# A fused attention and gated MLP kernel: every pair of head groups runs its sums and values together, and the whole written order is replaced

## The chip, the cores and the metric

The kernel runs on one core of one Trainium2 chip. The metric is the device time of one execution in microseconds (us). Three runs of the kernel before took 283.26, 287.59 and 288.25 us, so the median is 287.59 us and the runs differ by 1.7% among themselves. One further execution was recorded by the hardware profiler; its records span 282.1 us.

A core has five engines, each with a queue of its own: TensorE (PE, with weight loads as PEld), VectorE (DVE), ScalarE (ACT), GpSimd (POOL) and SyncE (SP), which here only issues transfers. Transfers between the outer memory, SBUF and back are done by 16 DMA engines.

## The reference

`B=8` batches, `H=12` heads, `S=448` positions, head dimension `D=64`. All inputs and the output are float32.

```python
q_n, k_n = rmsnorm(q, g_q), rmsnorm(k, g_k)        # x / sqrt(mean(x*x) + 1e-6) * g
scores = 1/sqrt(64) * q_n @ k_n.T                   # (8, 12, 448, 448)
attn = softmax(scores)
x = (attn @ v).transpose(0, 2, 1, 3).reshape(8, 448, 768)

h = maximum(x @ w_in, 0)                            # w_in (768, 1024)
u, v = h[..., :512], h[..., 512:]
v_n = (v - mean(v)) / sqrt(var(v) + 1e-6)           # over the 512
v_s = einsum('ts,bsd->btd', w_spatial, v_n) + b_spatial[None, :, None]
out = (u * v_s) @ w_out                             # w_out (512, 768)
```

## The kernel before

**Groups and units.** Four heads of one batch make a group `G`; there are 24 groups, three to a batch. A group's q, k or v is one tile of 128 partitions (two heads of 64 partitions, seven positions in each) by 2 x 448 numbers, 448 KB. A group's scores are made in seven units; a unit fills two PSUM banks with 128 x 448 numbers each.

**The order is written out by hand.** The string `PLAN` holds some 1,700 words. Each word is one step, `name.arguments/slots/engine`, and the loop at the end of the kernel (L722 to L725) calls `op_<name>` for each word. The scheduler of the language is off, so each engine runs its instructions in the order in which the words stand. What an engine does next is therefore fixed; a late operand holds everything behind it on the same engine. Waits are put in from the tiles that an instruction reads and writes. `SLOTS` (L160) says how many buffers of each kind there are; the slot numbers in the words choose among them. SP's transfers are issued in the order of the words as well.

**The words, in the order of the work of a group:**

- `L` loads q, k or v (L298; v of a group in the second half position goes in two halves, L304). `Q` squares (L391, L393), `R` sums the squares over a head (L404), `I` and `J` make 1/rms with a logarithm and an exponential on ACT (L417, L422), `N` multiplies (L437), on POOL or DVE. For group 0 the same steps exist by halves: `l q r i j n`.
- q and k must then be turned. `T` does it as a transposing transfer from SP (L492), after which k gets its factor g in `Z` (L473 on ACT, L475 on DVE). Or `P` does it on the PE (L456; `p` by halves, L464), and `K` (`k`) copies PSUM to SBUF, with the factor g for k.
- `S` makes the scores of one unit, eight matmuls of 64 x 32 weights (L517), which stand on eight different parts of the PE array. `E` is the exponential of a unit (L525, ACT), two banks at once.
- `s`, `a` and `b` are the passes: sums of the exponentials by a column of ones, and the two halves of the values (L550). A pass over one unit of one group is four matmuls of 64 x 32 weights. `flip` (L314) decides on which half of the partitions a group's heads lie. With groups below `SINGLES` (4) the flip is 0 and each pass is issued alone. From group 4 on, odd groups are flipped, and a pass of an even group and of the odd one after it are issued together (last argument 1): eight matmuls on eight parts of the array.
- `D` and `d` make 1/sum on ACT (L569, L573), `X` multiplies the values by it into `xt` (L579).
- For a batch: `V` and `U` are the two halves of x @ w_in (L595, L661), each in three steps of two matmuls; `c` and `u` the maximum with 0 (L586 on ACT, L588 on DVE); `B`, `M`, `m`, `A` the normalisation (L636, L637, L642, L645, L652); `H` the spatial product (L675), `G` the product with u (L680), `O` the last product (L689), `o` its copy to SBUF (L372 ACT, L374 DVE), `t` the store. `W` does the last 64 rows of V of a batch and of O of the batch before (L624).

**The weights.** `wi` loads w_in in eight transfers from POOL (L332), each 32 partitions of all three column groups; no `U` or `V` is placed before all eight. `ws` loads w_spatial early (L336); it is turned on the PE by `Y` (L359) and copied by `y`. `wb` and `wx` bring the bias into the last row.

**The factor g.** `gl` loads g_q and g_k as two rows into one partition, issued by SP behind the loads of group 0 (L307). `gA` multiplies them (L378), `gB` turns the row into a column with a small float32 matmul (L383), `gC` copies the column to `g2_col` (L386). Every `k`, `K` and `Z` reads `g2_col`.

**Fill work.** `z` issues matmuls of the identity (L263), 159 in all in 42 words, each of 64 columns, written into the unused 64 columns of PSUM bank 7.

Of the kernel before, what the change touches and what calls it, by code (L numbers as in the profile page):

```python
# [9 lines left out]
FP = mybir.dt.float32  # L10
# [26 lines left out]
S.2.3/34 E.2.1/h/a s.0.3.0 L.5.1/5 s.1.6.0 wi.0.0//g F.1//v P.3.1/7 P.3.0/6 E.2.3/i/a D.0/0/a Q.4.1/1/v R.4.1//v
I.4//a S.2.6/34 F.2//g b.1.3.0/0 b.1.0.0 D.1/1/a b.1.4.0 b.1.6.0 K.3.0/3/v wi.1.0//g s.2.1.0/6 b.1.2.0 d.0//a
b.2.1.0/5 E.2.6/j/a b.2.3.0 Q.5.1/0/g K.3.1/3/v J.4//a b.2.2.0 a.1.6.0/7 L.5.0/6 Q.5.0/2/a X.0.0//v N.4.1/2/g d.1//a
a.1.4.0 a.1.0.0 R.5.1//v a.2.3.0/4 N.4.0/3/g S.2.4/23 E.2.4/k/a R.5.0//v I.5//a b.2.5.0 b.1.1.0 b.2.0.0 X.0.1//v  # L40
a.2.6.0 b.1.5.0 s.2.0.0 a.2.5.0 J.5//a X.1.1//v a.1.1.0 S.3.0/23 E.3.0/l/a s.2.2.0 s.2.4.0 s.2.6.0 s.2.5.0 s.2.3.0
a.1.2.0 b.2.4.0 D.2/0/a S.3.3/01 E.3.3/9/a S.3.5/23 a.1.5.0 a.2.4.0 Q.6.0/1/g a.1.3.0 b.2.6.0 X.1.0//v E.3.5/1/a
a.2.0.0 N.5.0/0/g d.2//a N.5.1/1/g z.0/f a.2.1.0 a.2.2.0 R.6.0//v S.3.2/01 S.3.1/67 U.0.0.0/3 U.0.3.1/2 U.0.0.1
X.2.0//v V.0.0.1/4 L.6.1/8 Q.6.1/0/a X.2.1//v U.0.3.0 L.8.1/7 T.4.1/0 V.0.1.0/5 Z.4/0/v E.3.1/c/a Q.8.1/2/g E.3.2/2/a
U.0.0.2 u.0.0//a T.4.0/0 S.4.3/67 E.4.3/a/a R.6.1//v L.7.0/4 S.3.4/01 E.3.4/0/a V.0.0.2 I.6//a V.0.1.1 V.0.0.0
c.0.0//v V.0.1.2 c.0.1//v U.0.3.2 S.4.1/67 J.6//a S.4.4/01 S.4.5/34 wx//a W.0/5 E.4.1/8/a B.0.0//v S.4.2/67 u.0.3//v
Q.7.0/1/g E.4.4/b/a L.3.2/2 S.3.6/01 U.0.2.1/2 E.4.5/4/a N.6.1/2/g U.0.1.2/4 U.0.2.2 E.4.2/5/a U.0.2.0 T.5.0/1 F.3//v
S.4.6/67 s.3.2.0/3 E.3.6/f/a E.4.6/g/a s.3.5.0 T.5.1/1 Z.5/1/v c.0.3//v N.6.0/3/g S.5.1/01 s.3.0.0 u.0.2//v E.5.1/i/a
s.3.4.0 a.3.0.0/2 S.5.6/67 R.7.0//v E.5.6/7/a b.3.5.0/5 s.3.1.0 L.7.1/3 b.3.4.0 S.4.0/01 E.4.0/6/a L.8.0/0 R.8.1//v
a.3.2.0 s.3.6.0 Q.7.1/0/g b.3.0.0 L.9.0/9 s.3.3.0 a.3.5.0 D.3/1/a B.0.3//v b.3.6.0 Q.8.0/1/g R.7.1//v S.5.4/67  # L50
E.5.4/k/a Q.9.0/2/g wo//g S.5.5/01 B.0.1//v L.5.2/6 F.5//v U.0.1.1 L.4.2/5 V.0.2.1/3 E.5.5/3/a I.7//a F.4//g V.0.2.0
V.0.2.2 U.0.1.0 S.5.3/67 s.4.5.1/10 c.0.2//v d.3//a J.7//a u.0.1//a s.4.1.1 s.4.4.1 s.4.6.1 B.0.2//v T.6.1/0 S.5.2/34
E.5.3/j/a a.3.4.0 a.3.3.0 Z.6/2/v T.6.0/2 S.5.0/67 a.3.1.0 N.7.0/0/g b.3.3.0 E.5.2/e/a E.5.0/h/a b.3.2.0 L.10.0/8
S.6.3/34 s.4.3.1 a.3.6.0 b.3.1.0 a.4.4.1/76 R.8.0//v I.8//a E.6.3/d/a M.0//a a.4.0.1 m.0//a s.4.2.1 s.4.0.1 D.5/0/a
X.3.1//v a.4.3.1 a.4.5.1 N.7.1/1/g a.4.6.1 X.3.0//v R.9.0//v S.6.2/34 D.4/1/a b.4.0.1/52 b.4.3.1 d.5//a b.4.5.1
E.6.2/l/a b.4.2.1 a.4.2.1 A.0.2//v L.9.1/2 A.0.3//v b.4.6.1 T.7.1/1 A.0.1//v T.7.0/3 b.4.4.1 a.4.1.1 b.4.1.1 A.0.0//v
X.5.1//v S.6.0/01 H.0.2/3 H.0.0/2 d.4//a X.4.1//v G.0.2//v E.6.0/1/a X.4.0//v S.6.4/45 S.6.6/01 V.1.1.1/7 H.0.1/3
Q.9.1/0/g X.5.0//v J.8//a V.1.1.0 Q.10.0/1/a E.6.4/0/a L.10.1/1 S.6.1/45 Z.7/3/v R.9.1//v E.6.6/9/a I.9//a N.8.0/2/g
N.8.1/3/g S.7.6/01 G.0.0//v J.9//a E.6.1/2/a N.9.1/1/g V.1.1.2 R.10.0//v V.1.2.1/2 G.0.1//v V.1.2.2 E.7.6/f/a V.1.2.0
U.1.0.1/3 c.1.2//v B.1.2//v S.7.0/45 Q.10.1/2/a S.7.5/01 L.11.0/6 L.11.1/5 Q.11.1/0/g H.0.3/6 G.0.3//v R.10.1//v  # L60
E.7.0/c/a L.8.2/4 E.7.5/6/a U.1.0.0 c.1.1//a U.1.0.2 F.8//g S.7.2/45 E.7.2/h/a T.8.0/0 S.7.3/01 E.7.3/a/a u.1.0//v
W.1/726 o.0.3.1/0/a S.6.5/45 N.9.0/0/g S.7.1/01 T.8.1/0 V.1.0.2/3 V.1.0.1 E.6.5/j/a E.7.1/3/a o.0.3.0//v S.7.4/45
V.1.0.0 T.9.1/1 c.1.3//v B.1.1//v E.7.4/4/a O.0.0.0/6 Z.8/0/v S.8.2/01 S.8.1/45 s.6.3.1/72 I.10//a s.6.4.1 L.7.2/3
s.6.6.1 s.6.1.1 B.1.3//v c.1.0//a E.8.2/5/a E.8.1/e/a Z.9/1/v o.0.0.0/1/v Q.11.0/1/g R.11.1//v s.6.2.1 J.10//a s.6.5.1
s.6.0.1 L.6.2/0 D.6/1/a d.6//a D.7/0/a S.8.0/01 B.1.0//v L.14.1/7 U.1.2.0/3 R.11.0//v U.1.1.0/6 T.9.0/1 M.1//a U.1.1.2
d.7//a F.7//g N.10.0/2/g m.1//a U.1.1.1 L.12.0/2 U.1.2.1 U.1.2.2 u.1.1//v F.6//a u.1.2//v O.0.1.1/4 o.0.1.1/2/a
E.8.0/7/a N.10.1/3/v O.0.1.0/7 U.1.3.1/3 U.1.3.2 U.1.3.0 I.11//a S.8.5/56 S.9.1/01 a.6.3.1/42 A.1.3//v L.13.1/4
J.11//a o.0.1.0//a A.1.2//v u.1.3//v a.6.1.1 A.1.1//v A.1.0//v E.8.5/g/a T.10.1/0 Q.14.1/2/v b.6.2.1/73 b.6.4.1
N.11.1/1/g b.6.6.1 b.6.0.1 b.6.5.1 S.8.3/56 E.9.1/b/a E.8.3/k/a b.6.1.1 b.6.3.1 X.6.1//v S.9.2/01 a.6.2.1 a.6.5.1
a.6.4.1 a.6.0.1 X.7.1//v E.9.2/8/a a.6.6.1 X.6.0//v S.8.6/56 E.8.6/i/a X.7.0//v O.0.2.1/7 N.11.0/0/g S.9.4/01  # L70
o.0.2.1/3/a R.14.1//v E.9.4/2/a Z.10/2/v S.9.3/34 E.9.3/3/a S.9.6/56 H.1.0/2 Q.13.1/0/g L.13.0/9 E.9.6/a/a H.1.1/0
L.9.2/3 G.1.0//v Q.13.0/1/g G.1.1//v O.0.0.1/7 o.0.0.1//v S.8.4/34 S.9.0/56 Q.12.0/2/a S.9.5/12 H.1.3/7 T.11.1/1
# [85 lines left out]
"""  # L158


SLOTS = dict(raw=10, sqt=3, nrm=4, qT=4, kr=2, kT=4, et=22, rc=2, vs=2, vn=2, us=2, os=5)


@with_exitstack
def kernel(
# [17 lines left out]
    NG = 3  # L183
# [63 lines left out]

    def setup():
        dve.memset(eps, 1e-6)
        dve.memset(one_f, 1.0)  # L250
        dve.memset(ident, 0.0)
        make_identity(nc, ident)
        dve.memset(ones, 1.0)
# [502 lines left out]
```

## Time and profile before

| what | value |
|---|---|
| runs | 283.26, 287.59, 288.25 us |
| span of the profiled execution | 282.1 us |
| time of the profiled execution beside its span | not given; the fastest run is 1.1 us above the span, the median 5.4 us |
| mean granted clock of the PE | 0.967 |
| busy: PE, ACT, DVE, POOL | 263.9, 220.7, 207.0, 133.0 us |
| first and last exponential (L525) start | 16.0 and 235.0 us |
| chain that ended last | PE 74%, DVE 6%, ACT 6%, DMA 5%, issue 4% |

The page shows one execution. Busy time is the time in which an engine had at least one instruction under way. Matmuls lie on top of each other, so that a busy PE need not be a PE at its peak. The 40 slices cover some 7 us each, a digit is the busy share in tenths. The chain of work is followed back from the last instruction, at each step to what released it. "A <- B" behind an idle time says that A stood until B was done.

The execution has three stretches that differ: up to about 36 us few exponentials run and engines wait for loads; up to 236 us exponentials run nearly all the time, with the work of earlier batches between them; behind that the last two batches' MLP is done.

### The profile page before, as it was taken

The numbers are of one execution on the slowest core, as the hardware profiler recorded it, in microseconds if no ns is written. First come the engines' busy times: TensorE is split into PE (matmuls) and PEld (weight loads), VectorE is DVE, ScalarE is ACT, GpSimd is POOL, SyncE is SP. The second block draws the span as 40 slices with busy tenths as digits, with TensorE's granted clock in tenths as the row PEclk, the third lists the DMA queues.
The fourth block names the chain that finished last, engine by engine and source line by source line (L and its number), as shares of the span: only waits on it lengthen the run. The fifth ranks groups of instructions, "written<-read, shape, count | busy, mean of one in ns | idle before, by whom it ended". The sixth has DMA issues, their size and how long they took to land.

```text
span 282.1 us, 10242 instructions
## 1 busy us (share of the span) xinstructions
PE 263.9 (94%) x4408; PEld 141.6 (50%) x4408; DVE 207.0 (73%) x361; ACT 220.7 (78%) x361; POOL 133.0 (47%) x100
## 2 busy tenths in 40 slices
PE   7696999999799998999998997999999999999993
PEld 7574576345344544444444453444455546555551
DVE  5556777688799998789888776898689643656951
ACT  3529899999799999799998896997898997232332
POOL 2174799988297286373975545607571010000000
PEclk9757799999999999999999999999999999999999
DMA  6996677999999899999999999987334820243477
GB/s 150 352 332 222 194 158 137 248 291 240 202 263 237 230 183 374 181 253 226 281 245 235 267 252 228 213 216 268 65 67 97 208 94 2 58 139 78 119 193 228
DMA packets 63015, 56.64 MB, mean 201 GB/s; under 512 B 39545, under 2 KB 58618, under 8 KB 62970
## 3 DMA queue, kind: packets, MB, share of 16 engines
q1 hardware_dynamic: 61466, 53.23, 76.7%
q0 software_dynamic: 1504, 2.76, 5.6%
q8 instruction: 34, 0.56, 0.8%
q14 instruction: 11, 0.09, 0.1%
HBM read 38.55 MB, written 11.01 MB: 176 GB/s over the span
## 4 chain that ended last, share of the span: by engine, by line
PE 74%; DVE 6%; ACT 6%; DMA 5%; issue 4%; POOL 3%; SPq 1%; POOLq 0%; DVEq 0%
PE ps L550 17%; PE ps L661 13%; PE ps L517 12%; PE ps L689 11%; PE ps L595 8%; PE ps L675 7%; ACT et L525 3%; DMA g_row<-in_g_k_dram 2%; DMA raw<-in_v_dram 2%; PE ps L624 2%; PE ps L359 2%; DVE xt L579 1%; POOL nrm L437 1%; PE ps L456 1%; DVE ss L404 1%
## 5 line engine op out<-in xcount | busy, mean ns | idle before, releaser
L525 ACT ACTIVATE et<-ps 128x896 bf16<-128x896 f32 x168 | 145.2, 922 | 17.9 <-PE ps L517 12.8
L437 POOL TENSOR_TENSOR nrm<-raw,rs 128x896 bf16<-128x896 f32 x37 | 61.9, 1688 | 30.3 <-issue 8.5
L393 POOL TENSOR_TENSOR sqt<-raw 128x896 f32<-128x896 f32 (+1 forms) x30 | 49.4, 1654 | 33.7 <-DVE vn L652 14.6
L517 PE MATMUL ps<-qT,kT 64*32 64x448 bf16 x1344 | 58.5, 364 | 2.0 <-DVE qT L374 0.7
L404 DVE TENSOR_REDUCE ss<-sqt 128x14 f32<-128x896 f32 x46 | 48.9, 1075 | 2.5 <-ACT sqt L391 1.4
L550 PE MATMUL ps<-et,vt 64*32 64x448 bf16 x1344 | 46.6, 349 | 1.4 <-issue 1.4
L661 PE MATMUL ps<-xt,w_in 128*128 128x448 bf16 x192 | 43.2, 353 | 0.0
L595 PE MATMUL ps<-w_in,xt 128*128 128x512 bf16 x144 | 37.5, 380 | 3.4 <-issue 3.2
L689 PE MATMUL ps<-w_out,gt 128*128 128x384 bf16 x192 | 36.1, 326 | 0.3 <-DVE xt L579 0.2
L517 PEld LDWEIGHTS <-kT 64*32 64x32 bf16 x1344 | 20.9, 91 | 30.8 <-issue 21.4
L579 DVE TENSOR_TENSOR xt<-ps,rc 128x448 bf16<-128x448 f32 x48 | 27.3, 618 | 12.2 <-PE ps L550 7.7
L550 PEld LDWEIGHTS <-vt 64*32 64x32 bf16 x1344 | 24.8, 92 | 13.6 <-issue 3.0
L372 ACT ACTIVATE os<-ps 128x384 f32<-128x384 f32 (+1 forms) x34 | 16.4, 491 | 15.5 <-PE ps L689 13.6
L675 PE MATMUL ps<-w_spT,vn 128*128 128x448 bf16 (+1 forms) x128 | 27.8, 353 | 0.6 <-DVE xt L579 0.4
L661 PEld LDWEIGHTS <-w_in 128*128 128x128 bf16 x192 | 17.7, 98 | 19.1 <-issue 4.0
L326 POOL CAST vt<-raw 128x896 bf16<-128x896 f32 x15 | 14.0, 930 | 28.1 <-DMA raw<-in_v_dram 15.3
L550 PE MATMUL ps<-et,ones 64*32 64x448 bf16 x672 | 26.7, 352 | 0.0
L689 PEld LDWEIGHTS <-gt 128*128 128x128 bf16 x192 | 18.4, 98 | 15.2 <-issue 1.9
L680 DVE TENSOR_TENSOR gt<-ps,us 128x448 bf16<-128x448 f32 x32 | 19.4, 619 | 7.5 <-PE ps L675 6.4
L374 DVE COPY os<-ps 128x384 f32<-128x384 f32 (+1 forms) x30 | 16.4, 554 | 11.1 <-PE ps L689 4.9
L595 PEld LDWEIGHTS <-xt 128*128 128x128 bf16 x144 | 12.4, 97 | 21.8 <-issue 10.6
L636 DVE BATCH_NORM_STATS2 s<-vs 128x6 f32<-128x512 bf16 (+1 forms) x32 | 21.9, 684 | 1.0 <-ACT vs L586 0.6
(64 smaller groups left out, 270.1 us busy)
## 6 DMA issues: line engine op xcount, KB each, us to landing
out_dram<-os SPq DMA_DIRECT2D x55, 192.0 KB, 3.2
raw<-in_q_dram SPq DMA_DIRECT2D x23, 448.0 KB, 5.3
raw<-in_k_dram SPq DMA_DIRECT2D x23, 448.0 KB, 5.7
raw<-in_v_dram SPq DMA_DIRECT2D x14, 448.0 KB, 6.1
raw<-in_v_dram SPq DMA_DIRECT2D x20, 224.0 KB, 5.7
w_in<-in_moe_w_in_dram POOLq DMA_DIRECT2D x8, 192.0 KB, 6.2
w_out<-in_moe_w_out_dram POOLq DMA_DIRECT2D x1, 768.0 KB, 9.2
raw<-in_k_dram SPq DMA_DIRECT2D x2, 224.0 KB, 4.6
```

What stands on the lines that cost most here:

```text
L393: port(eng, eng.tensor_tensor(out=t, in0=x, in1=x, op=ALU.mult))
L404: dve.tensor_reduce(out=sss[G % 3][:, i].rearrange("p r c -> p (r c)"), in_=sqt[where.pop(("sq", G, i))].rearrange("p r (c d) -> p (r c) d ...
L437: port(eng, eng.tensor_tensor(out=nrm[sl[0]].rearrange("p c r d -> p r c d"), in0=raw[where["raw", G, i]].rearrange("p r (c d) -> p r c d" ...
L517: pe.matmul(out=ps[at:at + 32, sl[n], 0:S], lhsT=kT[64 * r:64 * r + 64, c, 64 * hh + 32 * x:64 * hh + 32 * x + 32], rhs=qT[64 * r:64 * r + ...
L525: act.activation(out=ets[sl[0]], in_=ps[:, a:b + 1:b - a, 0:S], func=AF.Exp, bias=0.0, scale=1.0)
L550: pe.matmul(out=ps[32 * l:32 * l + 32, where[kind, G][0], 0:S], lhsT=w, rhs=et_of(G, r, c)[at:at + 64], start=(n == 1), stop=(n == C), til ...
L579: dve.tensor_tensor(out=xts[b % 2][:, 2 * g + half, :], in0=ps[:, where.pop(("ab"[half], G))[0], 0:S], in1=rcs[where["rc", G]], op=ALU.mult)
L595: pe.matmul(out=ps[:, bank, :], lhsT=xts[b % 2][:, j, 128 * m:128 * m + 128], rhs=w_in[:, j % 2, j // 2, DH:], start=(n == 1 and j == 2 * ...
L636: dve.bn_stats(out=s6, in_=vss[b % SLOTS["vs"]][rows, m, :])
L661: pe.matmul(out=ps[:, bank, 0:S], lhsT=w_in[:, j % 2, j // 2, 128 * f:128 * f + 128], rhs=xts[b % 2][:, j, :], start=(n == 1 and j == 2 * ...
L675: pe.matmul(out=ps[:, sl[0], 0:S], lhsT=vns[b % SLOTS["vn"]][rows, m, 128 * f:128 * f + 128], rhs=w_spT[rows, m, :], start=(m == 0), stop= ...
L689: pe.matmul(out=ps[:, sl[0], 0:384], lhsT=gts[b % 2][:, f, 128 * m:128 * m + 128], rhs=w_out[:, f, 384 * h:384 * h + 384], start=(f == 0), ...
```

## The change

1. `SINGLES` goes. All odd groups are flipped (`SECOND`), so groups 0 to 3 are paired in `s`, `a` and `b` too, and v of groups 1 and 3 is loaded in two halves.
2. g_q and g_k are loaded as columns straight into 128 partitions, two transfers issued by ACT; one DVE instruction (`gp`) makes `g2_col`. `gA`, `gB`, `gC` go.
3. w_in is loaded in six transfers, each of 128 partitions and one column group; `U` and `V` need only the part that they read. w_spatial is loaded later, and the bias goes through a buffer of `rc`; its copy is done on POOL.
4. The fill matmuls are of 448 columns and 44 in number, 36 of them at the start.
5. `PLAN` is new from end to end: which engine does a step, which slot and bank it uses, and its place. 35 instead of 40 of the turns are transfers, 11 instead of 6 are on the PE. Of the multiplications `N` 16 instead of 9 are on DVE. Of the `c` and `u`, 32 instead of 22 are on ACT.

```diff
-SINGLES = 4
+SECOND = {1, 3, 5, 7, 9, 11, 13, 15, 17, 19, 21, 23}
 
 PLAN = """
-setup//v z.0/f z.3/f z.1/f l.1.0/0 q.1.0/0/v r.1.0//v z.0/f l.0.0/1 z.1/f q.0.0/1/a z.3/f r.0.0//v i.0//a j.0//a z.2/f
-L.1.0/2 z.2/f z.1/f n.0.0//v Q.1.0/2/a z.1/f z.3/f z.1/f z.1/f z.12/f l.0.1 n.1.0//v z.1/f z.2/f gl.0//s z.1/f z.6/f
...
+l.1.1/0 setup l.0.0/1 l.0.1 z.36/0 gl.1//a l.1.0 gl.0//a L.1.1/2 L.1.0/3 L.3.0/4 q.1.1/0/g L.2.0/5 L.2.1/6 q.0.0/1/a
+r.1.1 L.3.1/7 q.0.1//a r.0.0 L.7.1/8 r.0.1 L.4.1/9 q.1.0//a gp i.1//a r.1.0 i.0//a j.0//a j.1//a n.0.0//v Q.1.1/2/a
+n.1.0//v p.0.0/0 R.1.1 n.1.1//g p.1.0/1 Q.1.0/1/a n.0.1//g L.4.0/0 p.1.1/2 R.1.0 Q.3.0/0/a L.3.2/1 p.0.1/3 k.1.0/0/v
+I.1//a z.3/4 J.1//a k.0.0/0/v k.1.1//a N.1.1/0/g k.0.1//v S.0.0/45 z.1/6 Q.2.0/2/a S.0.4/67 S.0.1/01 z.1/2 E.0.4/0/a
+ws Q.2.1/1/v L.5.1/2 P.1.1/2 E.0.0/1/a S.0.3/36 R.2.0 z.1/7 N.1.0/1/g E.0.3/2/a S.0.6/47 R.2.1 E.0.1/3/a S.0.5/35
...
-    g_row = const.tile([1, 2, 2, D], FP, name="g_row")
-    g2_row = const.tile([1, 128], FP, name="g2_row")
+    g_col = const.tile([128, 2], FP, name="g_col")
     g2_col = const.tile([128, 1], FP, name="g2_col")
...
-    def dummies(bank, n):
-
-        out = ps[:, bank, 0:128] if bank < 8 else ps[:, bank - 8, S:S + 64]
+    def op_z(sl, e, n):
+
         for _ in range(n):
-            pe.matmul(out=out, lhsT=ident, rhs=ident[:, 0:128 if bank < 8 else 64], start=True, stop=True)
-
+            pe.matmul(out=ps[:, sl[0], 0:S].rearrange("p (c t) -> p c t", c=C), lhsT=ident,
+                      rhs=ident[:, None, 0:T].to_broadcast([128, C, T]), start=True, stop=True)
...
     def op_gl(sl, e, i):
         x = (g_q, g_k)[i]
-        engines[e].dma_start(out=g_row[:, i], in_=bass.AP(tensor=x.tensor, offset=x.offset, ap=[[0, 1], [0, 2], [1, D]]))
+        engines[e].dma_start(out=g_col[:, i:i + 1], in_=bass.AP(tensor=x.tensor, offset=x.offset, ap=[[0, 2], [1, D]]))
+
+    def op_gp(sl, e):
+        dve.scalar_tensor_tensor(out=g2_col, in0=g_col[:, 0:1], scalar=scale, in1=g_col[:, 1:2],
+                                 op0=ALU.mult, op1=ALU.mult)
...
     def flip(G):
-        return G % 2 if G >= SINGLES else 0
+        return int(G in SECOND)
...
-    def op_wi(sl, e, half, l):
-        x = bass.AP(tensor=moe_w_in.tensor, offset=moe_w_in.offset + (64 * l + 32 * half) * DF,
-                    ap=[[DF, 32], [256 * DF, NG], [1, DF]])
-        pool.dma_start(out=w_in[32 * l:32 * l + 32, half, :, :], in_=x)
-        where["wi", half, l] = True
+    def op_wi(sl, e, half, g):
+        x = bass.AP(tensor=moe_w_in.tensor, offset=moe_w_in.offset + (256 * g + 32 * half) * DF,
+                    ap=[[64 * DF, 4], [DF, 32], [1, DF]])
+        pool.dma_start(out=w_in[:, half, g, :], in_=x)
+        where["wi", half, g] = True
...
     def op_wb(sl, e):
-        sync.dma_start(out=oss[-1][64:65, 0:S], in_=moe_b_spatial.rearrange("(o s) -> o s", o=1))
-        where["wb"] = True
+        where["wb"] = sl[0]
+        sync.dma_start(out=rcs[sl[0]][64:65, :], in_=moe_b_spatial.rearrange("(o s) -> o s", o=1))
...
-    def op_gA(sl, e):
...
-    def op_gB(sl, e):
...
-    def op_gC(sl, e):
...
-            assert where["x", b, j] and all(where["wi", h, l] for h in range(2) for l in range(4))
+            assert where["x", b, j] and where["wi", j % 2, j // 2]
```

More of the change, by code (lines that the diff above doesn't have):

```diff
@@ L158 @@
 """
-SLOTS = dict(raw=10, sqt=3, nrm=4, qT=4, kr=2, kT=4, et=22, rc=2, vs=2, vn=2, us=2, os=5)
+SLOTS = dict(raw=10, sqt=3, nrm=4, qT=4, kr=2, kT=4, et=22, rc=2, os=5, vs=2, vn=2, us=2)
 @with_exitstack
@@ L605, in op_W @@
         if b < B:
-            assert all(where["x", b, j] for j in range(6))
+            assert all(where["x", b, j] and where["wi", j % 2, j // 2] for j in range(6))
             where["V", b, 3] = sl[0:1]
```

266 lines of the change are left out of this document (121 added, 145 removed).

## The prediction

> **What bounds the kernel now.** I read the page's busy shares and slices first, then the stages, then the start of ACT in order of time, and last the chain.
>
> ```profile
> span 282.1 us, 10242 instructions
> PE 263.9 (94%) x4408; PEld 141.6 (50%) x4408; DVE 207.0 (73%) x361; ACT 220.7 (78%) x361; POOL 133.0 (47%) x100
> ACT  3529899999799999799998896997898997232332
> PE 74%; DVE 6%; ACT 6%; DMA 5%; issue 4%; POOL 3%; SPq 1%; POOLq 0%; DVEq 0%
> ```
>
> The chain is three quarters PE, but ACT's slices are 6 to 9, mostly 8 and 9, from the 4th to the 35th: while exponentials run, two engines are close to full. The exponentials mark the stages:
>
> ```profile
> L525 ACT ACTIVATE et<-ps x168: 899/917/986, 16.0 to 235.0; 128x896 bf16<-128x896 f32 x168
> ...
> 15.99 0.90 ACT L525 ACTIVATE et<-ps 128x896 bf16<-128x896 f32 x1
> 21.07 0.92 ACT L525 ACTIVATE et<-ps 128x896 bf16<-128x896 f32 x1 [4.18 <-PE ps L263]
> ...
> 34.31 5.76 ACT L525 ACTIVATE et<-ps 128x896 bf16<-128x896 f32 x7
> ```
>
> Counting these rows and those between (1, 1, 3, 1, 1, 3, 1, 1), the group at 34.31 is numbers 13 to 19, so the 14th ends at about 36.0. The group also gives the pace of back-to-back exponentials: (5.76 - 0.92) / 6 = 0.81 us, 0.88 of the duration of one, since one starts before the last has ended. I cost all ACT work at 0.88 of its mean duration.
>
> So there are three stages: **start** to the 14th exponential, 36.0 us; **middle** to the end of the last exponential at 235.9 us, 199.9 us; **tail**, 46.2 us. For the middle I counted the steps that stand in the written order between the two exponentials and gave each its group's mean: ACT 211.6 us x 0.88 = 186 us, so ACT idles some 14 us there. PE, with 0.19 us per `S` or pass, comes to some 180 us. Both could set the pace, ACT a little more.
>
> ```profile
> 30.00:70.00 40.00, 39.63 (x774) 22.56 (x776) 30.28 (x46) 38.64 (x62) 34.14 (x26) 0.98 0.95 219
> ```
>
> In this stretch groups 0 to 3 make their unpaired passes (behind the comma: PE, PEld, DVE, ACT, POOL, clock). ACT is busy 38.6 of 40 us. What PE saves here cannot shorten these 40 us by more than 1.4.
>
> **The change part by part.** *Paired passes.* Rows of the chain, start, length, what:
>
> ```profile
> 43.38 1.51 PE ps L550 x32
> 65.70 0.76 PE ps L550 x32
> 99.56 0.69 PE ps L517 x24
> 117.24 2.27 PE ps L595 x10
> ```
>
> The first is eight unpaired passes of four matmuls, 0.19 us each; the second is four paired ones of eight, 0.19 us too. A pair costs what a single costs. The words for passes go from 294 to 252: 42 x 0.19 = 8.0 us of PE. It is not 8.0 us of span, by the paragraph above; it becomes room in which other PE work is done earlier. In the new order the middle has 34 fewer passes (-6.5), but 5 more `P` (0.45 each by the row below, +2.2), 3 `Y` from the start (half of the last row's 1.20 at full clock, +1.8), 2 more `H` (0.76, +1.5), 3 `O` (0.65, +2.0) and 3 steps of `V` (0.45 by the row of L595 above, +1.4): +2.4 us, some 1% of PE's middle, inside ACT's.
>
> ```profile
> 39.37 0.89 PE ps L456 x14
> 239.39 0.76 PE ps L675 x4
> 240.15 0.65 PE ps L689 x4
> 13.84 1.20 PE ps L359 x14
> ```
>
> *Tail.* PE fills it: its work behind the last exponential sums to 40.3 us, and it runs from 235.9 to the end of the row of 276.56 at 277.4. The new order has there 2 `H`, 3 `O` and 3 `V` less, 3 passes more: -1.5 - 2.0 - 1.4 + 0.6 = **-4.3 us**. It now ends with a full block, not with the 64-row one: two stores of 192 KB in place of a 96 KB one, 3.2 instead of 2.6 us to land: **+0.6 us**.
>
> ```profile
> 276.56 0.81 PE ps L624 x8
> 277.38 0.54 DVE os L374
> out_dram<-os SPq DMA_DIRECT2D x55, 192.0 KB, 3.2
> out_dram<-os SPq DMA_DIRECT2D x2, 96.0 KB, 2.6
> ```
>
> *ACT in the middle.* By engine in the two orders, ACT gets 5 more `c`, 4 `u` and 3 `K`, and one `Q`, one `Z` and `wx` less.
>
> ```profile
> L586 ACT ACTIVATE us<-ps 128x448 bf16<-128x448 f32 x10 | 5.5, 550 | 4.0 <-PE ps L661 3.9
> L586 ACT ACTIVATE vs<-ps 128x512 bf16<-128x512 f32 x8 | 4.8, 598 | 2.5 <-PE ps L595 2.5
> L473 ACT ACTIVATE kT<-kr,g_col 128x896 bf16<-128x896 bf16 x3 | 3.1, 1044 | 0.0
> L372 ACT ACTIVATE w_spT<-os 1x448 bf16<-1x448 f32 x1 | 1.0, 1026 | 0.0
> L391 ACT ACTIVATE sqt<-raw 128x896 f32<-128x896 f32 x12 | 11.4, 955 | 3.8 <-DMA raw<-in_q_dram 3.7
> L437 DVE TENSOR_TENSOR nrm<-raw,rs 128x896 bf16<-128x896 f32 x9 | 9.7, 1084 | 3.1 <-POOL nrm L437 1.9 <-issue 1.2
> ```
>
> 5 x 0.60 + 4 x 0.55 + 3 x 1.0 - 0.96 - 1.04 - 1.03 = 5.2 us, x 0.88 = **+4.6 us**, all on the pacing engine. DVE gets 7 more `N` in the middle (+7.6) but loses 4 `c`, 4 `u` and 4 `Z`; counted like ACT its durations there grow by 3 us, to some 177 as they stand, and it stays under ACT. POOL loses 7 `N`. The ACT idle of 14 us I leave as it is.
>
> *Start.* Before, three things hold: g, the second exponential, and PE at a low clock.
>
> ```profile
> 0.00:10.00 10.00, 7.13 (x135) 6.92 (x135) 4.15 (x13) 2.93 (x5) 1.41 (x7) 1.00 0.78 201
> 10.00:20.00 10.00, 8.70 (x92) 6.57 (x93) 6.55 (x9) 5.13 (x10) 5.18 (x7) 0.56 1.06 363
> 20.00:30.00 10.00, 7.70 (x112) 5.30 (x109) 6.52 (x10) 8.15 (x12) 5.97 (x6) 0.67 0.67 189
> 3.36 0.62 DVE L393 TENSOR_TENSOR sqt<-raw 128x448 f32<-128x448 f32 x1 [1.13 <-DMA raw<-in_k_dram]
> 10.49 0.76 DVE L378 SCALAR_TENSOR_TENSOR g_row<-g_row 1x128 f32<-1x128 f32 x1 [3.54 <-DMA g_row<-in_g_k_dram]
> 13.29 0.66 DVE L475 TENSOR_SCALAR kT<-ps,g_col 64x896 bf16<-64x896 bf16 x1
> 14.97 2.44 PE L517 MATMUL ps<-qT,kT 64*32 64x448 bf16 x24
> L404 DVE TENSOR_REDUCE ss<-sqt 128x14 f32<-128x896 f32 x46 | 48.9, 1075 | 2.5 <-ACT sqt L391 1.4
> ```
>
> 201 GB/s over ten microseconds is 2.0 MB. The new order puts the four 224 KB parts of group 0 first and group 1's k and q behind them, 1.8 MB, with no w_spatial among them: the last of these lands at about 10. From there `Q.1.0` 0.96, `R` 1.07, then `k.1.0`, `k.0.0`, `k.0.1` at some 0.65 each, and an `S` at the low clock 0.8 (2.44 / 3): first exponential at about 14.8, hardly earlier than 16.0. But by then both halves of group 0 are turned, so all seven of its units follow without a stop, and the fill matmul on which the second one stood (4.18 us, L263) has gone from its bank. 14 exponentials at 0.81 give 11.3 us, with the two pairs of `I`, `J` between them some 12: the 14th ends at 27 to 28 instead of 36.0: **-8 us**. Bounds: -10 if g and the loads land as quickly as the first load (in time for 3.36), -2 if something on this road is as late as now. `gp` stands in DVE ahead of `r.1.0`, and that holds `i`, `j` and all `n`: g's two transfers, now 128 pieces each, must land by 7 us or the start moves with them; no row shows a load of that form, the nearest took to 10.4, behind 1.1 MB on SP, and would cost 3 us.
>
> ```profile
> raw<-in_k_dram SPq DMA_DIRECT2D x23, 448.0 KB, 5.7
> ```
>
> The six w_in transfers carry the same bytes and are not needed before 60 us; two more half loads of v are two more issues in SP's queue, and the loads behind them move with them. I cost both at nothing: a load stands 8 us of ACT work ahead of its use (median of the written order, least 3.3) and lands in 5.7; where that cover is gone, `Q` on POOL or ACT waits, which is the slow rival's way. [...]
>
> The chain has `S` between full-array work at 24 matmuls in 0.69 us, 0.12 above 3 x 0.19. [...]
>
> **Sum**: 282.1 - 8 (start) + 4.6 (ACT, middle) - 4.3 (tail) + 0.6 (end) = **275.0 us of span**. The three runs have a mean of 286.4, 4.3 above the profiled span (1.1 to 6.1); with 4.3 the time is **279.3 us**, 2.9% below the median of 287.59.
>
> **The rivals.** *Transposing transfers come late (slower).*
>
> ```profile
> kr<-nrm SPq DMA_TRANSPOSE x20, 4.3
> DMA to landing us min/median/max: 2.9/4.5/8.5
> ```
>
> The second row is that of all transfers of L492, k and q. Measured in ACT work between the words, the new order puts most `T` of q 3 to 7 us, and of k 4 to 6 us, ahead of what reads them. A median landing fits; one of 8.5 us holds `Z` on DVE for up to 4.5 us, behind it stand `R`, `X` and the next `S`, and with those the exponentials. Against it: five turns fewer are transfers. Sign turns when this costs 8.2 us (to the median), 2% slower at about 14 us: three or four full-length landings with nothing to hide them. Then 275.0 + 14 + 4.3 = 293 us.
>
> *The start gains nothing* (g late, loads late, or PE at half clock): -2 instead of -8, 281.0 of span, 285.3 us. For it: the clock rows, 0.56 and 0.67 while PE was busy 8.7 and 7.7 of 10; at 15 us 24 matmuls of `S` took 2.44 us, later 0.69. [...] Worked out from rows: up to the 28th exponential the new order has 14 us of PE work at full rate, 29 at half, against 28 us of exponentials and other ACT work from the first on: at most some 3 us late.
>
> *PE's room also ends ACT's waits*: half of the 14 us goes, 268 of span, 272 us. For it: exponentials stood 12.8 us for `S`.
>
> ```profile
> ACT et L525 <- PE ps L517: 12.8, 20, 1.9
> ```
>
> Against it: they did so all along, most of it where passes are paired already.
>
> **How the numbers follow.** Forecast 0.50, start gains nothing 0.22, transfers late 0.20, waits end too 0.08. Range: from the last case, 271, to a start without gain and the largest distance from span to run, 281.0 + 6.1 and rounding, 288; it leaves out most of the slow case. About 2% is what these runs can tell from no change. Faster by over 2% (under 281.8): the forecast less some 0.06 of its upper part, and the last case, 0.52. Within 2%: 0.28. Slower: 0.20.
>
> **What would show it.** Start: the 14th exponential ends near 28, none of them stands for L263's successor. Middle: about 204 us from there to the last exponential, ACT busy 190 of them. Tail: 42 to 43 us, PE full. Passes: L550's successor with 252 x 8 matmuls, 0.19 us per eight. Wrong, if `Z` or `S` stand for transfers (L492's successor) for more than 8 us together, or if ACT idles over 22 us in the middle.

## The result and the profile after

| what | before | changed | ratio, 95% interval |
|---|---|---|---|
| time | 286.66 us (median) | 389.3 and 390.5 us | 1.373 (1.357 to 1.388) |
| span of the profiled run | 282.1 us | 387.5 us | |
| exponentials (L525 before, L501 after) stood | 17.9 us | 98.9 us | |

The change makes the kernel 37% slower; the forecast was 279.3 us. Two more runs of the changed kernel took 428 and 510 us at granted clocks of 0.716 and 0.549 and are left out of the comparison. The runs of both kernels end 1.7 to 1.8 us above their own spans, so the 4.3 us that the prediction put between the two was too much.

The page of the changed kernel, its busy shares, slices, chain and the row of the exponentials:

```profile
span 387.5 us, 10068 instructions
PE 298.7 (77%) x4311; PEld 139.7 (36%) x4326; DVE 208.9 (54%) x353; ACT 234.9 (61%) x371; POOL 123.3 (32%) x94
ACT  2886646557576653468566646648667666763422
PEclk9985656889899985799989989869999899999998
PE 64%; ACT 24%; issue 4%; DVE 4%; DMA 2%; SPq 0%; POOL 0%; another core or an unknown queue 0%; ACTq 0%; DVEq 0%; POOLq 0%
L501 ACT ACTIVATE et<-ps 128x896 bf16<-128x896 f32 x168 | 150.5, 916 | 98.9 <-PE ps L526 30.9
```

ACT's slices, mostly 8 and 9 before, are mostly 4 to 7 from the fourth on, and PE's share fell from 94% to 77%: neither engine is full. ACT's share of the chain rose from 6 to 24%. The view of waits says for whom they stand (line, releaser, us, times, longest):

```profile
ACT et L501 <- PE ps L526: 30.9, 28, 2.5
ACT et L501 <- PE ps L493: 28.3, 36, 1.8
PE ps L526 <- ACT et L501: 26.2, 28, 2.0
```

Before, of the 17.9 us that exponentials stood, 12.8 were for `S` and 4.2 for a fill matmul (L263); they never stood for a pass. Now the largest row is L526, the passes. An exponential reads the two banks of its unit, which hold its scores until then, and no pass writes those. In order of time the two engines wait for each other like this (start, length, what, in brackets the idle time before it):

```profile
47.22 2.10 PE L526 MATMUL ps<-et,vt 64*32 64x448 bf16 x40
49.38 0.92 ACT L501 ACTIVATE et<-ps 128x896 bf16<-128x896 f32 x1 [2.47 <-PE ps L526]
50.35 0.58 PE L526 MATMUL ps<-et,vt 64*32 64x448 bf16 x8 [1.04 <-ACT et L501]
```

ACT waits until a run of 40 pass matmuls is over, then PE waits until the exponential is over. By the order of the words this exponential is `E.2.4`. Its unit lies in banks 0 and 7 (`S.2.4/07`), and its scores were done at 47.4. The 40 matmuls are five words of the pass `a.0`, which write banks 5 and 4 (`a.0.5.1/54`); the pass behind it, `b.0.0.1`, writes banks 1 and 2. None of these is a bank that the exponential needs.

By the stages of the prediction: start 31.8 us (36.0 before), middle 312.1 (199.9), tail 43.6 (46.2). The stretch of the middle, of before and of the changed kernel (columns as in the prediction; behind the clock the share of the DMA engines and GB/s), and the changed kernel's first and last exponential:

```profile
36.00:235.90 199.90, 192.91 (x3626) 96.04 (x3622) 159.84 (x270) 184.68 (x297) 116.45 (x81) 1.00 0.93 210
```

```profile
31.80:343.90 312.10, 237.45 (x3722) 107.52 (x3730) 166.79 (x274) 198.05 (x306) 108.59 (x78) 0.88 0.59 135
...
L501 ACT ACTIVATE et<-ps x168: 897/917/939, 17.2 to 343.0; 128x896 bf16<-128x896 f32 x168
```

ACT is busy 198 of 312 us, PE 237, at a mean clock of 0.88. The exponentials themselves last 917 ns as before. The whole loss is in the middle: it is 112 us longer, of which ACT is busy for 13 and idle for the rest.

**Where the waits come from.** `E` reads both banks of its unit as one strided range, `ps[:, a:b + 1:b - a, 0:S]`. In the order before, the two are neighbours in all 168 units. In the new order they are neighbours in 40, and two to seven banks apart in 128 (`S.2.6/36`, `S.2.1/05`). I counted the semaphore waits in the two built programs: of the waits of exponentials on PE, none of 150 before and some 85 of 144 after are released by an instruction that writes none of the two banks, nearly always one *between* them. Of PE's waits on ACT, 2 of 219 before and more than half of 201 after are for an instruction that shares no bank with what waits. So the program treats the banks that are stepped over as read. This was there to be read in the slot numbers of the words.

### The profile page after: what moved, and what is told of

It is laid out like the page before. It is cut to its first block, busy times and chain, and to the rows that moved or that the text cites. A ratio compares the mean times of both kernels' runs of the same rounds, so it can differ in the third digit from the quotient of the medians.

```text
span 387.5 us, 10068 instructions
## 1 busy us (share of the span) xinstructions
PE 298.7 (77%) x4311; PEld 139.7 (36%) x4326; DVE 208.9 (54%) x353; ACT 234.9 (61%) x371; POOL 123.3 (32%) x94
## 3 DMA queue, kind: packets, MB, share of 16 engines
q0 software_dynamic: 3776, 2.77, 4.8%
## 4 chain that ended last, share of the span: by engine, by line
PE 64%; ACT 24%; issue 4%; DVE 4%; DMA 2%; SPq 0%; POOL 0%; another core or an unknown queue 0%; ACTq 0%; DVEq 0%; POOLq 0%
ACT et L501 23%; PE ps L526 16%; PE ps L493 11%; PE ps L637 10%; PE ps L665 8%; PE ps L571 7%; PE ps L651 6%; PE ps L600 3%; DMA raw<-in_k_dram 2%; PE ps L432 1%; DVE xt L555 1%; PE ps L347 1%; DVE ss L380 0%; DVE nrm L413 0%; SPq L300 0%
## 5 line engine op out<-in xcount | busy, mean ns | idle before, releaser
L501 ACT ACTIVATE et<-ps 128x896 bf16<-128x896 f32 x168 | 150.5, 916 | 98.9 <-PE ps L526 30.9
L493 PE MATMUL ps<-qT,kT 64*32 64x448 bf16 x1344 | 69.3, 399 | 24.2 <-ACT et L501 20.4
L413 POOL TENSOR_TENSOR nrm<-raw,rs 128x896 bf16<-128x896 f32 x30 | 50.5, 1686 | 91.2 <-ACT rs L398 43.5
L526 PE MATMUL ps<-et,vt 64*32 64x448 bf16 x1344 | 57.0, 415 | 15.0 <-ACT et L501 14.9
L637 PE MATMUL ps<-xt,w_in 128*128 128x448 bf16 x192 | 48.0, 372 | 8.1 <-ACT et L501 8.0
L493 PEld LDWEIGHTS <-kT 64*32 64x32 bf16 x1344 | 22.5, 95 | 59.0 <-issue 54.6
L526 PE MATMUL ps<-et,ones 64*32 64x448 bf16 x672 | 32.2, 409 | 11.2 <-ACT et L501 11.2
L665 PE MATMUL ps<-w_out,gt 128*128 128x384 bf16 x192 | 38.1, 334 | 3.4 <-ACT et L501 3.2
L526 PEld LDWEIGHTS <-vt 64*32 64x32 bf16 x1344 | 23.8, 104 | 35.9 <-issue 30.2
L651 PE MATMUL ps<-w_spT,vn 128*128 128x448 bf16 (+1 forms) x128 | 29.9, 364 | 4.3 <-ACT et L501 4.3
L637 PEld LDWEIGHTS <-w_in 128*128 128x128 bf16 x192 | 17.9, 100 | 31.7 <-issue 20.1
L315 POOL CAST vt<-raw 128x896 bf16<-128x896 f32 x17 | 15.5, 931 | 42.3 <-DMA raw<-in_v_dram 33.6
```

Of the source, the lines that this page charges most:

```text
L413: port(eng, eng.tensor_tensor(out=nrm[sl[0]].rearrange("p c r d -> p r c d"), in0=raw[where["raw", G, i]].rearrange("p r (c d) -> p r c d" ...
L493: pe.matmul(out=ps[at:at + 32, sl[n], 0:S], lhsT=kT[64 * r:64 * r + 64, c, 64 * hh + 32 * x:64 * hh + 32 * x + 32], rhs=qT[64 * r:64 * r + ...
L501: act.activation(out=ets[sl[0]], in_=ps[:, a:b + 1:b - a, 0:S], func=AF.Exp, bias=0.0, scale=1.0)
L526: pe.matmul(out=ps[32 * l:32 * l + 32, where[kind, G][0], 0:S], lhsT=w, rhs=et_of(G, r, c)[at:at + 64], start=(n == 1), stop=(n == C), til ...
L637: pe.matmul(out=ps[:, bank, 0:S], lhsT=w_in[:, j % 2, j // 2, 128 * f:128 * f + 128], rhs=xts[b % 2][:, j, :], start=(n == 1 and j == 2 * ...
L651: pe.matmul(out=ps[:, sl[0], 0:S], lhsT=vns[b % SLOTS["vn"]][rows, m, 128 * f:128 * f + 128], rhs=w_spT[rows, m, :], start=(m == 0), stop= ...
```

## The experiments

Theory A: these false waits (waits for a bank that the instruction does not use) cost the 105 us of span between before and changed. Rivals: the new order, the pairing, or the late transfers of w_in. "Start", "middle" and "tail" are the stages of the prediction.

**Neighbouring banks (e1) and both banks apart (e2).** Only bank numbers in the words change, of the units and of what else uses PSUM, in the changed order (e1) and in the order before (e2). Two words of e1:

```diff
-S.2.1/05
-S.2.6/36
+S.2.1/12
+S.2.6/34
...
```

> The changed kernel with nothing but other PSUM bank numbers: every unit of scores gets two neighbouring banks (in the changed kernel 128 of 168 units have one to six banks between their two). Theory A, waits on the banks between: the exponential reads both banks as one strided range, and the program makes it wait for, and hold up, work in the banks between. Then the 312 us of the middle fall to 205 to 215, and the span is 32 + 210 + 44 = 286 us at most, likelier 280. Theory B, the new order itself (late transfers, tight order, low clock): bank numbers change nothing much, span 375 to 395.

Measured: 294.9 us, ratio 1.034 (1.026 to 1.042); start 30.4, middle 220.8, tail 42.7. 93.6 us of span are gone, but it is above the 286 expected. The largest thing that exponentials stood for in e1 is `S` again; for passes they stood 0.2 us:

```profile
ACT et L501 <- PE ps L493: 20.5, 28, 6.3
```

> The kernel before with nothing but other bank numbers: the two banks of every unit 3 to 7 apart. Theory A: counted in the program, 100 of 138 waits of exponentials on PE are then for a bank between (86 of 144 in the changed kernel), so the span goes from 282 to 360 to 430 us, with the clock lower. Theory B: it stays within 2% of before.

Measured: 559.2 us, ratio 1.97 (1.95 to 1.98), further than the 360 to 430 expected. Its waits have the sign of the changed kernel; this is the largest row of the exponentials, which stood 246 us in all (L550 are the passes there):

```profile
ACT et L525 <- PE ps L550: 53.5, 34, 4.1
```

The same kind of edit takes nine tenths of the loss away in one order and makes a larger one in the other, so theory A holds for the size of the loss. New bank numbers alone cost some 10 us (c1 below), not this.

**The change's own banks, each exponential in two instructions (e3).**

```diff
-        act.activation(out=ets[sl[0]], in_=ps[:, a:b + 1:b - a, 0:S], func=AF.Exp, ...)
+        for n, bank in enumerate((a, b)):
+            act.activation(out=ets[sl[0]][:, n, :], in_=ps[:, bank, 0:S], func=AF.Exp, ...)
```

> The changed kernel, its banks as they are, each exponential issued as two instructions of one bank each, so that no instruction covers a range of banks. ACT pays: two of 448 numbers at some 0.55 x 0.88 are 0.97 us instead of 0.81, 168 times, 27 us. Theory A: 280 + 27 = 307 us of span, 295 to 320, in spite of the added work less than the changed kernel's 387. Theory B: 387 + 27 or more.

Measured: 291.4 us, ratio 1.025 (1.019 to 1.030), span 288.1, below the 295 to 320 expected. Splitting is cheap: in order of time of e3, eight halves (four units) take 3.57 us, where four whole ones take 3.32 to 3.35:

```profile
21.03 3.57 ACT L502 ACTIVATE et<-ps 128x448 bf16<-128x448 f32 x8
```

And exponentials hardly stand for passes any more (one wait of 1.6 us); the row of all of them:

```profile
L502 ACT ACTIVATE et<-ps 128x448 bf16<-128x448 f32 x336 | 159.2, 606 | 10.1 <-PE ps L493 8.0
```

With no bank number changed, 99 us are gone. 13 us remain to the forecast of 275.0.

**Unpaired again (e4).** e1 with groups 0 to 3 not flipped, passed singly, v of groups 1 and 3 loaded whole.

```diff
-SECOND = {1, 3, 5, 7, 9, ...}
+SECOND = {5, 7, 9, ...}
```

> As the first of these runs, neighbouring banks, but groups 0 to 3 unflipped and their passes issued singly (42 passes of four matmuls more, 8.0 us of PE at 0.19). By the prediction ACT paces this stretch, so it costs 0 to 4 us against the first run. If PE paces it, the whole 8 us.

Measured: 291.2 us, 1.024 (1.019 to 1.030), span 289.3: against the expectation not slower than the paired e1 but some 4 us faster. That could not be read alone, for both lose time between 48 and 68 us, e1 more: from 50 to 60 us PE is busy 8.0 us in e4 and 3.9 in e1. Stretches of e1 (behind the comma: PE, PEld, DVE, ACT, POOL, clock, DMA share, GB/s), and PE there in order of time:

```profile
50.00:60.00 10.00, 3.90 (x120) 1.84 (x105) 7.48 (x10) 5.64 (x10) 2.81 (x3) 0.81 1.16 116
60.00:70.00 10.00, 9.10 (x61) 2.51 (x61) 1.99 (x3) 3.78 (x7) 2.07 (x2) 0.68 0.87 197
```

```profile
60.50 2.29 PE L571 MATMUL ps<-w_in,xt 128*128 128x512 bf16 x5 [4.47 <-DMA w_in<-in_moe_w_in_dram]
```

From 50 to 60 us PE and ACT are busy 3.9 and 5.6 us, and ACT only 3.8 in the ten behind, while the DMA engines are busy and move 116 GB/s. The same ten microseconds of the kernel before:

```profile
50.00:60.00 10.00, 9.67 (x120) 3.92 (x121) 6.59 (x13) 9.67 (x14) 8.33 (x6) 1.00 1.14 284
```

In e1, loads issued at 52 to 57 us need 14 to 16 us to land. Three of the six transfers of w_in are issued at 49 to 51, and one of the six takes 17.8 us. The changed kernel itself does not show it: its first `V` comes at 70.4 us, that of e1 at 55.6.

**w_in: shape or place (e5, e6, e7).** All three on e1: the eight transfers of before at the new places (e5), the six transfers all behind `wx` (e6), the eight behind `wx` (e7).

```diff
# e5, e7
-            ap=[[64 * DF, 4], [DF, 32], [1, DF]])
-        pool.dma_start(out=w_in[:, half, g, :], in_=x)
+            ap=[[DF, 32], [256 * DF, NG], [1, DF]])
+        pool.dma_start(out=w_in[32 * l:32 * l + 32, half, :, :], in_=x)
# e6 (e7 with its eight words)
-wx//g P.3.0/5 ... wi.0.1 ... wi.0.0 ... wi.1.0 ... wi.1.1 ... wi.0.2 ... wi.1.2
+wx//g wi.0.1 wi.0.0 wi.1.0 wi.1.1 wi.0.2 wi.1.2 P.3.0/5 ...
```

> The changed order with neighbouring banks (span 293.9 us), with w_in in the eight transfers of the kernel before (32 partitions by three column groups), at the same places of the order. Theory of the shape: from 49 to 67 us the DMA engines are busy above 1.0 and move only some 110 GB/s, because the six transfers go as 3,072 packets of 512 bytes instead of 768 of 2 KB; with the old shape loads issued at 52 to 57 us land in 5 to 8 us instead of 15, PE does not stand at 50 to 58, and the span is 281 to 285. Rival, the place: whatever their shape, transfers issued at 47 to 51 us are too late for the first step of V; then PE still stands for them and the span is 289 to 294.

> The changed order with neighbouring banks, the six transfers of w_in as the change has them, but all issued one behind the other at 34 to 38 us instead of 34 to 51. Theory of the shape: the slow stretch moves to 36 to 52 us, loads issued there land late, and the span stays within 4 us of 293.9, at most some 5 us better because fewer loads are issued there. Theory of the place: all six have landed by about 50 us, nothing stands for them, and the span is 281 to 285.

> Both: eight transfers, all issued at 34 to 39 us. Either theory: 280 to 285 us of span. If it is below the one with eight transfers at the old places by over 3 us, place has a price of its own. If it stays at 289 or above, w_in is not what holds the changed order, and the wait of POOL for the multiplications on DVE (13.8 us) is.

Measured spans: 293.3, 287.7 and 283.6 us; medians 295.8, 292.8 and 287.9 us; ratios 1.034 (1.025 to 1.043), 1.022 (1.011 to 1.033), 1.023 (1.012 to 1.034). At the late place the shape is worth nothing: eight transfers land in 5.2 us in the median, but one still in 11.7, and PE stands for them (e5):

```profile
PE ps L571 <- DMA w_in<-in_moe_w_in_dram: 7.8, 2, 5.8
```

e6 fits neither of its two theories: 287.7 lies between the 281 to 285 of the place and the 289 or more of the shape. Its six transfers take 13.3 us to land in the median, those of e7 6.1. So the shape counts at the early place. The early place alone is worth 6 us by the spans of the traced runs (e1 to e6) and 2 by the medians, the shape there another 4 to 5 (e6 to e7). Both edits together are worth 10.3 us of span (e1 to e7), and 7.8 with a second run of e7 (e10):

> The version with neighbouring banks and w_in in eight early transfers once more, as the measure for the other two of this call: span 281 to 286, time 284 to 290.

Measured: 288.3 us, 1.014 (1.009 to 1.020), span 286.1; start 30.2, middle 213.1, tail 42.8. e7 and e10 are one program, so their ratios, 1.023 and 1.014, show how little a difference of 1% between two ratios says.

**Are my bank numbers free? (c1, c2, e8, e9).** c1 gives the kernel before new bank numbers by the same means as e1, c2 by a second means that avoids taking a bank too soon after its last use; e8 and e9 use the second means for e1 and e7. Only bank numbers change.

> Control: the kernel before with its bank numbers drawn anew in the same way, every unit on neighbouring banks as it has them already. If renumbering by itself costs nothing, the time is within 1% of before; if it costs 1 to 3%, a part of what the changed order with neighbouring banks loses is owed to my numbers and not to its order.

> Control: the kernel before, its banks drawn anew a second time, every unit on neighbouring banks, now so that a bank is taken again only where the step before it on that bank is likely to be over. Theory: the 10 us that the first control lost were the price of my first numbers (exponentials stood 23.2 us for S instead of 12.8), so this one is within 1% of before, its exponentials stand for S at most 15 us, and the span is 280 to 285. Rival: any numbers other than the ones that the order was made with cost 2 to 3%.

> The changed order, w_in as the change has it, every unit on neighbouring banks with numbers drawn in the same second way. Theory: 3 to 8 us below the first renumbered version (293.9), because that one paid for my first numbers: span 286 to 291. The stop at 49 to 67 us for the transfers of w_in stays. Rival: the numbers are not what it loses, span 292 to 295.

> The changed order with w_in in eight transfers at 34 to 39 us and the second numbers. If false waits, my first numbers and the place of w_in are all that kept the change from its forecast, the span is 274 to 279 and the time 278 to 283, 1 to 3% faster than before. If the order has yet another loss in the middle, the span stays at 280 to 284 and the time is the same as before within 2%.

Measured: c1 1.028 (1.018 to 1.038), span 292.1; c2 1.007 (1.001 to 1.012), span 282.6. The rows of both:

```profile
ACT et L525 <- PE ps L517: 23.2, 31, 2.3
```

```profile
ACT et L525 <- PE ps L517: 16.6, 24, 2.5
```

So a poor set of numbers costs the order before 10 us, all in the middle (210.1), and a good one 0.1 to 1.2%. For the changed order the second means did not help: e8 1.052 (1.043 to 1.060), span 294.3, no better than e1; e9 1.032 (1.023 to 1.042), span 290.4, 4 to 7 us *above* e10 and e7. Both expectations failed, and I cannot say what numbers that are free of cost would give there.

**Pairing, and the change's own numbers with w_in early (e11, e12).** e11 is e7 unpaired as in e4; e12 is e3 with the eight early transfers.

> The same with groups 0 to 3 unpaired again (no flip, single passes, v of groups 1 and 3 in one load). With the stop for w_in gone, the price of pairing can be seen: if PE paces the middle (busy 202.6 of 210.6 us there), the 42 single passes more cost 42 x 0.19 = 8 us, less what falls outside; span 4 to 8 us longer than the paired one. If ACT paces it, as the forecast had it, or if the passes lie in stretches in which PE waits anyhow, the difference is below 2 us.

> The changed order with its own bank numbers, each exponential in two instructions of one bank (so no bank between is waited for), and w_in in eight early transfers. My bank numbers have no part in it. If they are what is left of the loss, the span is 275 to 279. If the order itself is too long in the middle, the span is 280 to 284. ACT does some 7 us more here: if ACT paced the middle, it would be 285 and more.

Measured: e11 1.020 (1.015 to 1.024), span 287.7, PE busy 269.6 us against 265.8 in e10. Single passes put 3.8 us on PE and 1.6 us on the span; the intervals of the two ratios overlap, so the 1.6 is hardly clear of nothing. That is the second case of the expectation, below 2 us. The pages of e10 and e11:

```profile
PE 265.8 (93%) x4326; PEld 132.7 (46%) x4326; DVE 207.0 (72%) x353; ACT 226.7 (79%) x371; POOL 123.7 (43%) x96
```

```profile
PE 269.6 (94%) x4326; PEld 136.3 (47%) x4326; DVE 206.1 (72%) x353; ACT 226.8 (79%) x371; POOL 123.8 (43%) x96
```

e12: 285.0 us, 1.005 (1.002 to 1.008), span 283.6, the second case of its expectation (280 to 284): my bank numbers have no part in it, and it is still too long in the middle. With the false waits gone and w_in in eight early transfers, 103.9 of the 105.4 us between changed and before are gone.

**Which engine paces the middle? (e13, c3).** Two of four matmuls of each `O` are left out in e12 and in the kernel before, so that only PE has less to do.

```diff
-        for f in range(4):
+        for f in (0, 3):
```

> The version with two instructions for an exponential and w_in in eight early transfers, with two of the four matmuls of each O left out (half of the product u * v_s with w_out is missing in the output, except for the last 64 rows). No other engine's work changes. In the middle (209.9 us, PE busy 204.7) there are 56 x 0.16 = 9.1 us of PE less. If PE paces the middle, it becomes 201 to 204 us; if ACT does (busy 197.1), 208 to 210. The tail loses some 6 us either way.

> The kernel before with the same two of four matmuls of each O left out (half of that product is missing). In its middle (199.9 us, PE busy 192.9, ACT 184.7) there are 50 x 0.16 = 8.2 us of PE less. The forecast held that ACT paces there: then the middle stays at 197 to 200. If PE paces it too, it becomes 192 to 195.

The middles of e12, e13 and c3 (columns as above):

```profile
31.10:241.00 209.90, 204.69 (x3777) 103.37 (x3777) 163.99 (x273) 197.05 (x460) 109.82 (x80) 0.98 0.87 202
```

```profile
30.40:239.60 209.20, 199.41 (x3700) 98.47 (x3718) 163.24 (x273) 196.23 (x459) 109.81 (x80) 0.98 0.89 203
```

```profile
35.50:236.00 200.50, 189.89 (x3569) 93.62 (x3574) 159.13 (x270) 184.26 (x297) 116.05 (x80) 0.99 0.92 210
```

209.2 after 209.9, and 200.5 after 199.9: with 8 to 9 us of PE matmuls less, neither traced middle is shorter by more than 0.7 us, though PE was recorded busy for over 96% of the middles of e12 and before. PE's recorded busy time there falls by 5.3 and 3.0 us only. For e12 the times bear it out: e13 took 280.9 us in the median, some 4 less, and in its trace 2.7 of them are in the tail (some 6 expected) and 0.7 in the start. So the amount of PE work does not set the length of e12's middle. For the kernel before it is one trace: c3 was run twice, 280.4 us (traced, its tail 4.0 us shorter) and 276.0 us, and in which stage the second gained is not known. So c3 does not settle the middle of the kernel before.

**Less splitting (e14, e15).** e14 is e12 with a split only where the banks are no neighbours; e15 has a third set of numbers, 160 of 168 units neighbouring.

```diff
-        for n, bank in enumerate((a, b)):
-            act.activation(...)
+        if b == a + 1:
+            act.activation(out=ets[sl[0]], in_=ps[:, a:b + 1, 0:S], func=AF.Exp, ...)
+        else:
+            for n, bank in enumerate((a, b)):
+                act.activation(out=ets[sl[0]][:, n, :], in_=ps[:, bank, 0:S], func=AF.Exp, ...)
```

> The changed order with its own bank numbers and w_in in eight early transfers; an exponential is split only where its two banks are not neighbours (128 of 168 units), 40 go as one instruction again. Two halves take 0.90 us where one whole takes 0.81, so ACT does 40 x 0.05 to 40 x 0.09 = 2 to 3.6 us less. If ACT paces this version's middle (209.9 us), the span falls by 1 to 3 us, to 280 to 283; if it does not, it stays at 283 to 285.

> The same, its bank numbers drawn a third time, now from the change's own ones: 160 of 168 units on neighbouring banks, eight split. Nearly all of the price of splitting goes (7 us of ACT). If numbers can be had that cost the changed order nothing, the span is 276 to 280 and the time 1 to 2.5% below before. If it is 284 or more, neighbouring banks cost this order about what splitting does, and the forecast's 275 is out of its reach with these two means.

Measured: e14 285.1 us, 0.996 (0.993 to 1.000), span 283.3; e15 289.5 us, 1.011 (1.007 to 1.016), span 287.5. ACT is busy 1.6 us less in e14's middle (195.5), and that middle is no shorter (210.2). e15 is the last case of its expectation, its span 4.2 us above that of e14; whether neighbouring banks cost that or this set of numbers is not known.

The stages side by side, in us (from the rows of exponentials and of stretches of each run):

| run | start | middle | tail | span | ACT busy in the middle |
|---|---|---|---|---|---|
| before | 36.0 | 199.9 | 46.2 | 282.1 | 184.7 |
| changed | 31.8 | 312.1 | 43.6 | 387.5 | 198.1 |
| e1 neighbouring banks | 30.4 | 220.8 | 42.7 | 293.9 | 190.2 |
| e3 split | 30.3 | 215.5 | 42.3 | 288.1 | 196.6 |
| e10 neighbouring, w_in early | 30.2 | 213.1 | 42.8 | 286.1 | 190.2 |
| e12 split, w_in early | 31.1 | 209.9 | 42.6 | 283.6 | 197.1 |
| e14 split where needed | 30.7 | 210.2 | 42.4 | 283.3 | 195.5 |
| forecast | 28 | 204.5 | 42.5 | 275.0 | 190 |

## Why the prediction was wrong

**The step that failed is "The ACT idle of 14 us I leave as it is".** In the changed kernel it is 312.1 - 198.1 = 114 us. Beneath it lies item 5 of the change, "which slot and bank it uses", for which the sum has no term: the exponentials of 128 of 168 units now also wait for work in the banks between their two, and without these waits 99 us of span are gone (e3). None of the rivals held it. The test "if ACT idles over 22 us in the middle" caught it; "if `Z` or `S` stand for transfers" did not (`Z` 0.7 us), and the transposing transfers (L468) landed sooner than the 4.5 us of before, so that rival had no part. Who waited for them, and how long they took to land:

```profile
DVE kT L451: 0.7, 1
...
DMA to landing us min/median/max: 2.9/3.5/6.5
```

**"I cost both at nothing" (w_in and the loads).** The cover was "not needed before 60 us". In the changed kernel the first `V` starts at 70.4 and nothing stands for w_in, though the last transfer is issued at 58. With the false waits gone the first `V` comes up at 55.6 (e1), and the transfers are issued up to 51: then six late transfers in place of eight early ones cost 4.5 us of span (e3 to e12) to 10 (e1 to e7). This is the slow rival's kind of mechanism with other transfers.

**Start: -8 forecast, -4 to -6 measured.** The first exponential came at 17.2, not 14.8. Two rows of the changed kernel, ACT and POOL in order of time:

```profile
9.56 0.58 ACT L367 ACTIVATE sqt<-raw 128x448 f32<-128x448 f32 x1 [3.09 <-DMA raw<-in_k_dram]
```

```profile
12.71 1.83 POOL L421 TENSOR_TENSOR nrm<-raw,rs 128x448 bf16<-128x448 f32 x2 [8.44 <-DVE nrm L421]
```

The last quarter of group 0 lands at 9.5, as late as I put group 1's loads, and two of the four multiplications stand one behind the other on POOL, at 0.93 us where I had counted none. g landed at 9.8, later than the 7 us demanded, but only 0.3 us behind that quarter, so it cost nearly nothing. From the first exponential to the end of the 14th it took 14.6 us where the sum had some 12, with stops for PE and for `qT` between them.

**What held.** Tail: 42.3 to 44.1 us in the versions of the changed order without false waits, 42.5 forecast. ACT's own additions: busy 190 us in the middle of e1 and e10, 190 forecast. Paired passes are "not 8.0 us of span": 1.6 by e11. The reason given, that ACT paces the middle, is not shown: PE does not pace that of e12, but taking ACT work away (e14) did not shorten it either. The rival "the start gains nothing" on the clock did not come: PE was granted the full clock from 10 to 20 us, where it had 0.56 before; that the 36 wide fill matmuls did it was not tested. (The prediction's reading of ACT's slices runs one too far: they are high from the 4th to the 34th.) Stretches of the changed kernel:

```profile
0.00:10.00 10.00, 8.35 (x32) 3.81 (x33) 3.21 (x11) 2.88 (x4) 1.63 (x7) 1.00 0.75 202
10.00:20.00 10.00, 7.38 (x89) 3.64 (x90) 8.55 (x11) 8.88 (x16) 6.05 (x6) 1.00 1.07 353
```

**What stays open.** e12 is 8.6 us above the forecast span: 3.1 in the start, 5.4 in the middle. Splitting adds 7 us of ACT work there, which would be all of it if ACT paced that middle; e14, which took 1.6 us of it back and gained nothing, does not bear that out, and e13 excludes PE's work alone. Numbers without false waits and without a price were found for the order before, not for the new one. So whether this order could reach 275 us isn't settled. None of the versions that do all the work beats the kernel before by more than the measurement can tell; e14 is level with it.

## What to carry to other kernels

When an order is drawn anew, read its buffer numbers as part of the change: in this program the exponentials, which read two banks as one strided range, also waited for work in the banks between (some 85 of 144 waits on PE were for other banks, none of 150 before), and it is worth counting, in both orders, how many units are not neighbours. A pair that cannot be neighbours is better read by two instructions: here that takes 0.89 instead of 0.83 us of ACT, back to back, and saves the false waits (99 us of span in e3). When a large wait goes, look again at every transfer that was free because the kernel was slow.

## What the runs showed of the hardware

The two traces in which PE stood most, of the changed kernel and of e2, have the lowest mean granted clock. In the traces of before and of the changed kernel it is either 1.00 or 0.50, so a mean tells the time at half clock. The changed kernel, with PE busy for 77% of its span, had a mean of 0.892: some 85 us at half clock, in eleven stretches all along. The kernel before (94%, 0.967) had some 20 us in three, two of them in its start. e2 (66%) had 0.738, at these two values some 295 us. The traced runs of the changed order without false waits (90 to 94%) had 0.967 to 0.985. The 40 pass matmuls shown above lie in a stretch at 0.50: they take 2.10 us, 0.42 for eight, where eight took 0.19 before. So part of the 105 us may be PE running slower behind the false waits; how much was not taken apart. What makes the clock go back and forth was not shown.

From 50 to 60 us of e1 the DMA engines were busy 1.16 of their share and moved 116 GB/s, where the kernel before moved 284 at 1.14. In that stretch were a transposing transfer, four of the w_in transfers and five loads. The software queue handles 3,776 packets in the changed kernel where it had 1,504 before, for the same bytes (2.77 and 2.76 MB). By the packets in these two traces, w_in goes as 768 packets of 2,048 bytes in both, so the 512 bytes that I expected for e5 were wrong; what is new are 2,272 packets of 4 bytes. While the six transfers of the changed kernel run, most often 4 of the w_in packets are in flight at once; with the eight of before it is 16 or 17. That fits the longer landings (8.1 to 11.9 us in the changed kernel, 9.5 to 17.8 in e1, 4.8 to 7.9 before). It is not the whole of the slow stretch, for e5, with 1,504 packets again, stands as long there (189 GB/s from 50 to 60 us).
